# Window attention with a highway layer: fp32 loads by the hardware queue, fp16 conversion and causal masks on GpSimd, VectorE's highway sums kept in PSUM

## The chip, the cores and the metric

The kernel runs on one core of one Trainium2 chip. The metric is the device time of one execution in microseconds (us). A "fast" run is one whose time is within 1.5% of the fastest run of the same kernel; slower runs, which showed a lower granted clock in several cases (the granted clock is the share of TensorE's full clock that the profiler recorded), are called slow and are not compared with fast ones.

## The reference

Attention over a causal window of 128 positions plus 4 "sink" positions at the start of each sequence, and then a highway layer on the 3072 tokens.

```python
# q, k, v: (B=4, H=8, S=768, D=64) fp32; w_h, w_t: (512, 512); b_t: (512)
scores = q @ k.transpose(0, 1, 3, 2) / sqrt(D)
keep   = is_sink | ((rel >= 0) & (rel < 128))
a      = softmax(where(keep, scores, -1e9))
x      = (a @ v).transpose(0, 2, 1, 3).reshape(3072, 512)
Hh     = maximum(x @ w_h, 0)
T      = sigmoid(x @ w_t + b_t)
out    = T * Hh + (1 - T) * x            # (3072, 512) fp32
```

## The kernel before

The work is cut into 24 blocks of 128 rows, six per batch. Per block, `stage_T` transposes q and k, `stage_S` makes the scores and their exponentials `e`, `stage_mask` masks them, `stage_A` multiplies them with V, `stage_X` transposes the result `xh`, and `stage_Mt` and `stage_Mh` are the two matrix products of the highway layer (`tps` for the gate, `hps` for the highway side). Most tiles lie in SBUF; the matrix products are written to tiles in PSUM, where `ps_m` has two buffers for four kinds of tiles. In blocks 2 to 5 of a batch the sinks lie outside the window and are added by `stage_sink`, from two small block-diagonal tiles, `ks_bd` and `vs_bd`. These tiles are filled once per batch by ten small copies within SBUF (`stage_sink_setup`). They are the "sink copies".

```python
    AHEAD = 8
    NV = AHEAD + 3                                   # V ring
    m_ps = tile_pool("ps_m", bufs=2, PSUM)           # shared by tp, tps, hps, sk

    def load(n):                                     # software queue: converts fp32 to fp16
        nc.gpsimd.dma_start(out=qsd, in_=q[b, :, rows, :].transpose([1, 0, 2]))
        nc.gpsimd.dma_start(out=ksd, in_=k[b, :, rows, :].transpose([1, 0, 2]))
    def load_v(n):
        nc.gpsimd.dma_start(out=vt[:, :, 0:D], in_=v[b, :, rows, :].transpose([1, 0, 2]))
    # ... (cut: first loads, weights)
    bt32 = const.tile([1, DM], FP32, tag="bt32")
    nc.sync.dma_start(out=bt32, in_=moe_b_t.unsqueeze(0))          # bias: first DMA of SyncE

    def late_constants():                            # VectorE, in its fixed order
        # ... (cut)
        nc.vector.tensor_scalar_mul(bt16[0:1, :], bt32, 0.5)

    def stage_sink_setup(b):
        for hh in range(2):
            nc.sync.dma_start(out=ks3[rows, :, 4 * hh:4 * hh + NSINK],
                              in_=kT[rows, :, 0:NSINK])
        for h in range(H):
            nc.sync.dma_start(out=vs_bd[b % 2][r:r + NSINK, h // 4, h % 4, :],
                              in_=vt[0:NSINK, 65 * h:65 * h + 65])

    def stage_mask(n):
        for e in es:                                 # two tiles of 128x1024 (128x512 in block 0)
            nc.vector.tensor_tensor(out=ev, in0=ev, in1=m.to_broadcast(...), op=ALU.mult)

    def stage_Mh(n):
        # hps = xT @ wh, four matmuls
        nc.vector.scalar_tensor_tensor(out=dd, in0=hps, scalar=0.0, in1=xh, op0=ALU.max, op1=ALU.subtract)
        nc.vector.scalar_tensor_tensor(out=ee, in0=u, scalar=1.0, in1=dd, op0=ALU.add, op1=ALU.mult)
        nc.vector.scalar_tensor_tensor(out=otok, in0=xh, scalar=2.0, in1=ee, op0=ALU.mult, op1=ALU.add)
        nc.sync.dma_start(out=out[n * P:(n + 1) * P, :], in_=otok)

    with tc.manual_schedule(engines={ENG.PE, ENG.DVE, ENG.Activation}):
        for i in range(-2, NB + 1):
            # stage_sink(i), stage_S(i + 1), stage_A(i), stage_T(i + 2)
            # at each batch's first block: stage_sink_setup; at i == -2: late_constants()
            # loads of block i + 2 + AHEAD
            # stage_mask(i + 1), stage_Mt(i - 1), stage_X(i), stage_Mh(i - 1)
```

The softmax here doesn't subtract the row's maximum and nothing guards it: scores larger than these inputs give would overflow.

## Time and profile before

| | before |
|---|---|
| device time, median of 3 runs (range) | 137.16 us (136.8 to 137.25) |
| span of the profiled execution, granted clock | 134.9 us, 0.979 |
| first matmul of the highway product `hps` of block 0 / block 1 | 23.3 / 28.4 us |
| attention x V of block 2 | 25.3 us |
| `hps` of block 21 / last block | 121.7 / 128.1 us |

These are lines of the page of the kernel before: the busy shares of its engines, and, in 40 equal slices of the span (3.4 us each), tenths of busy time and the bytes moved; then the DMA queues with packets, megabytes and the time their packets took.

```profile
span 134.9 us, 3378 instructions
PE 117.1 (87%) x1312; PEld 73.6 (55%) x1312; DVE 108.5 (80%) x230; ACT 90.4 (67%) x129; POOL 65.7 (49%) x81
...
POOL 6999747889897789979489370000000000000000
...
GB/s 4 111 123 127 160 188 160 155 181 171 154 198 191 196 151 148 152 195 240 192 194 179 193 194 176 38 80 80 6 78 78 63 19 78 78 5 78 78 78 78
...
q0 software_dynamic: 75936, 10.49, 116.0%
q1 hardware_dynamic: 5890, 6.33, 14.6%
```

GpSimd (POOL) does little but issue loads, 0.9 us each, and is finished at 80 us.

The time from one block's `hps` to the next is called the pitch below, and an unusually long one a jump.

### The profile page before, as it was taken

Reading aid. Unit: us, or ns where it says so; the run is one execution under the profiler, and the core shown is the slowest. Engines: PE = TensorE matmul, PEld = TensorE weight load, DVE = VectorE, ACT = ScalarE, POOL = GpSimd, SP = SyncE. Lnnn points to the kernel's source line nnn. Section 1 sums busy time; section 2 is a strip of 40 time slices with the busy share of each in tenths; the row PEclk is TensorE's granted clock in tenths of the full one; section 3 lists DMA queues with packets and bytes.
Section 4 is the critical chain, followed back from the end, with each engine's and each line's share of the span. In section 5 each row is a group of like instructions: output and inputs, shape, how many; then the busy total and the mean of one; then the engine's idle time right before and its main releaser. Section 6 shows DMA issues by size and latency. Waiting matters only on the chain.

```text
span 134.9 us, 3378 instructions
## 1 busy us (share of the span) xinstructions
PE 117.1 (87%) x1312; PEld 73.6 (55%) x1312; DVE 108.5 (80%) x230; ACT 90.4 (67%) x129; POOL 65.7 (49%) x81
## 2 busy tenths in 40 slices
PE   6657939999999899999999899999998999999720
PEld 2225625856864466567565557656653685665300
DVE  6153724789988999899898998998989998999590
ACT  3054843779775977977777788779767977973310
POOL 6999747889897789979489370000000000000000
PEclk9999995999999999999999999999999999999996
DMA  0999999999999999999999999122011101101111
GB/s 4 111 123 127 160 188 160 155 181 171 154 198 191 196 151 148 152 195 240 192 194 179 193 194 176 38 80 80 6 78 78 63 19 78 78 5 78 78 78 78
DMA packets 81841, 17.02 MB, mean 126 GB/s; under 512 B 77729, under 2 KB 78753, under 8 KB 81826
## 3 DMA queue, kind: packets, MB, share of 16 engines
q0 software_dynamic: 75936, 10.49, 116.0%
q1 hardware_dynamic: 5890, 6.33, 14.6%
q8 instruction: 10, 0.16, 0.5%
q14 instruction: 5, 0.04, 0.1%
HBM read 20.97 MB, written 6.29 MB: 202 GB/s over the span
## 4 chain that ended last, share of the span: by engine, by line
DVE 33%; PE 32%; ACT 11%; issue 8%; POOL 7%; DMA 6%; DVEq 0%; POOLq 0%
PE hps L310 12%; ACT e L234 7%; DMA ksd<-in_k_dram 6%; DVE ee L316 6%; DVE otok L319 6%; DVE dd L313 6%; DVE e L247 5%; DVE xh L277 5%; PE tps L298 4%; PE xtp L286 4%; PE av L262 3%; DVE kT L186 3%; PE sk L211 3%; ACT qT L185 3%; POOL qsd L83 2%
## 5 line engine op out<-in xcount | busy, mean ns | idle before, releaser
L234 ACT ACTIVATE e<-sps,ebias 128x1024 f16<-128x1024 f32 (+1 forms) x48 | 47.4, 1039 | 11.2 <-PE sps L231 6.0
L298 PE MATMUL tps<-wt_sb,xT 128*128 128x512 f16 x96 | 25.5, 390 | 0.0
L310 PE MATMUL hps<-wh_sb,xT 128*128 128x512 f16 x96 | 24.7, 379 | 0.7
L83 POOL DMA_DIRECT2D qsd<-in_q_dram x24 | 21.6, 900 | 4.7 <-DMA wh_sb<-in_moe_w_h_dram 1.0
L84 POOL DMA_DIRECT2D ksd<-in_k_dram x24 | 21.4, 893 | 3.1 <-PE tp L182 1.3
L262 PEld LDWEIGHTS <-e 128*128 128x128 f16 x352 | 19.8, 98 | 3.2 <-issue 0.4
L301 ACT ACTIVATE u<-tps 128x512 f16<-128x512 f32 x24 | 14.4, 600 | 9.5 <-PE tps L298 9.5
L247 DVE TENSOR_TENSOR e<-e,mask 128x1024 f16<-128x1024 f16 x32 | 20.5, 682 | 0.0
L185 ACT COPY qT<-tp 128x512 f16<-128x512 f16 x24 | 14.0, 585 | 9.6 <-PE tp L182 9.6
L313 DVE SCALAR_TENSOR_TENSOR dd<-hps,xh 128x512 f16<-128x512 f32 x24 | 16.5, 688 | 4.1 <-PE hps L310 4.1
L186 DVE COPY kT<-tp 128x512 f16<-128x512 f16 x24 | 10.1, 423 | 11.7 <-ACT qT L185 11.7
L316 DVE SCALAR_TENSOR_TENSOR ee<-u,dd 128x512 f16<-128x512 f16 x24 | 16.6, 692 | 2.5
L319 DVE SCALAR_TENSOR_TENSOR otok<-xh,ee 128x512 f32<-128x512 f16 x24 | 16.6, 692 | 0.8
L277 DVE TENSOR_TENSOR xh<-av,rec 128x512 f16<-128x512 f32 x24 | 16.6, 691 | 0.8
L231 PE MATMUL sps<-qT,kT 64*128 64x128 f16 x352 | 15.4, 227 | 2.1 <-DVE kT L186 1.1
L231 PEld LDWEIGHTS <-kT 64*128 64x128 f16 x352 | 10.7, 98 | 9.5 <-issue 6.6
L288 ACT COPY xT<-xtp 128x512 f16<-128x512 f16 x24 | 14.0, 583 | 1.1 <-PE xtp L286 0.9
L298 PEld LDWEIGHTS <-xT 128*128 128x128 f16 x96 | 9.6, 100 | 9.1 <-issue 0.8
L310 PEld LDWEIGHTS <-xT 128*128 128x128 f16 x96 | 9.3, 98 | 8.6 <-issue 1.5
L286 PEld LDWEIGHTS <-xh 128*128 128x128 f16 x96 | 6.4, 101 | 13.4 <-DVE xh L277 11.2
L286 PE MATMUL xtp<-ident,xh 128*128 128x128 f16 x96 | 9.9, 228 | 3.8 <-DVE xh L277 3.8
L180 PE MATMUL tp<-ident,qsd 128*128 128x128 f16 x96 | 10.0, 231 | 2.4 <-DMA qsd<-in_q_dram 2.3
(88 smaller groups left out, 152.9 us busy)
## 6 DMA issues: line engine op xcount, KB each, us to landing
out_dram<-otok SPq DMA_DIRECT2D x24, 256.0 KB
qsd<-in_q_dram POOLq DMA_DIRECT2D x24, 128.0 KB, 7.3
ksd<-in_k_dram POOLq DMA_DIRECT2D x24, 128.0 KB, 7.4
wt_sb<-in_moe_w_t_dram POOLq DMA_DIRECT2D x1, 512.0 KB, 8.4
wh_sb<-in_moe_w_h_dram POOLq DMA_DIRECT2D x1, 512.0 KB, 10.1
v_91<-in_v_dram POOLq DMA_DIRECT2D x3, 128.0 KB, 8.0
v_92<-in_v_dram POOLq DMA_DIRECT2D x3, 128.0 KB, 6.1
v_93<-in_v_dram POOLq DMA_DIRECT2D x2, 128.0 KB, 8.0
```

Source lines behind the costliest of these rows:

```text
L83: nc.gpsimd.dma_start(out=qsd, in_=q[b, :, rows, :].transpose([1, 0, 2]))
L231: nc.tensor.matmul(sps[:, hh, o:o + P], lhsT=kk[rows, hp, :], rhs=qT[rows, hp, :], start=True, stop=True)
L234: nc.scalar.activation(out=e.rearrange("p a b c d -> p a (b c d)"), in_=sps[:, :, 0:2 * np_ * P], func=AF.Exp, bias=ebias, scale=SCALE)
L247: nc.vector.tensor_tensor(out=ev, in0=ev, in1=m.unsqueeze(1).to_broadcast([P, 4, np_ * P]), op=ALU.mult)
L262: nc.tensor.matmul(av[:, g, 2 * hl + hh, 0:_AVN], lhsT=es[g][:, hh, hl, pc, :], rhs=vt[:, 65 * h:65 * h + _AVN], start=first, stop=False, ...
L277: nc.vector.tensor_tensor(out=xh, in0=avh[:, :, 0:D], in1=rec.unsqueeze(2).to_broadcast([P, H, D]), op=ALU.mult)
L286: nc.tensor.transpose(xtp[:, j, :], xh[:, 2 * j:2 * j + 2, :], ident)
L298: nc.tensor.matmul(tps, lhsT=xT[:, kc, :], rhs=wt_sb[:, kc, :], start=False, stop=(kc == NOC - 1))
L310: nc.tensor.matmul(hps, lhsT=xT[:, kc, :], rhs=wh_sb[:, kc, :], start=(kc == 0), stop=(kc == NOC - 1))
L313: nc.vector.scalar_tensor_tensor(out=dd, in0=hps, scalar=0.0, in1=xh, op0=ALU.max, op1=ALU.subtract)
L316: nc.vector.scalar_tensor_tensor(out=ee, in0=u, scalar=1.0, in1=dd, op0=ALU.add, op1=ALU.mult)
L319: nc.vector.scalar_tensor_tensor(out=otok, in0=xh, scalar=2.0, in1=ee, op0=ALU.mult, op1=ALU.add)
```

## The change

The intent is to relieve VectorE. The masks become selects on GpSimd, which frees VectorE of 1.36 us per full block. To make room on GpSimd, the loads go to the hardware queue on SyncE. There the loads fill fp32 staging tiles, and GpSimd casts them to fp16. VectorE's two intermediate sums `dd` and `ee` stay in the PSUM tile `hps`, so that VectorE reads fewer SBUF operands beside GpSimd. The ring of V buffers shrinks from 11 to 6. The core of the diff (constants and the mask tile's shape are cut):

```diff
-    AHEAD = 8
+    AHEAD = 6
+    stage_pool = ctx.enter_context(tc.tile_pool(name="p_stage", bufs=AHEAD))
-    NV = AHEAD + 3
+    NV = 6
     def load(n):
+        for name, src in (("q", q), ("k", k), ("v", v)):
+            t = stage_pool.tile([P, H, D], FP32, tag=name + "32", name=name + "32")
+            nc.sync.dma_start(out=t, in_=src[b, :, rows, :].transpose([1, 0, 2]))
+            stage[name, n] = t
+    def cast(n):
-        nc.gpsimd.dma_start(out=qsd, in_=q[b, :, rows, :].transpose([1, 0, 2]))
-        nc.gpsimd.dma_start(out=ksd, in_=k[b, :, rows, :].transpose([1, 0, 2]))
+        nc.gpsimd.tensor_copy(out=qsd, in_=stage.pop(("q", n)))
+        nc.gpsimd.tensor_copy(out=ksd, in_=stage.pop(("k", n)))      # ScalarE for block 0
+        nc.gpsimd.tensor_copy(out=vt[:, :, 0:D], in_=stage.pop(("v", n)))
...
+    for n in range(AHEAD):
+        load(n)                                # 18 loads on SyncE, ahead of the bias
     bt32 = const.tile([1, DM], FP32, tag="bt32")
     nc.sync.dma_start(out=bt32, in_=moe_b_t.unsqueeze(0))
...
     def stage_mask(n):
-            nc.vector.tensor_tensor(out=ev, in0=ev, in1=m..., op=ALU.mult)
+            # c == 0: VectorE; c == 1: VectorE for the first half; else GpSimd for both halves
+            nc.gpsimd.affine_select(out=ev[:, :, 0, :], in_=ev[:, :, 0, :], ..., **keep_prev)
+            nc.gpsimd.affine_select(out=ev[:, :, 1, :], in_=ev[:, :, 1, :], ..., **keep_cur)
...
-        nc.vector.scalar_tensor_tensor(out=dd, in0=hps, scalar=0.0, in1=xh,
+        nc.vector.scalar_tensor_tensor(out=hps, in0=hps, scalar=0.0, in1=xh,
-        nc.vector.scalar_tensor_tensor(out=ee, in0=u, scalar=1.0, in1=dd,
+        nc.vector.scalar_tensor_tensor(out=hps, in0=u, scalar=1.0, in1=hps,
-        nc.vector.scalar_tensor_tensor(out=otok, in0=xh, scalar=2.0, in1=ee,
+        nc.vector.scalar_tensor_tensor(out=otok, in0=xh, scalar=2.0, in1=hps,
...
+            if i == -2:
+                cast(0); cast(1); load_weights(wt_sb, moe_w_t); cast(2); load_weights(wh_sb, moe_w_h)
+            elif i + 4 < NB:
+                cast(i + 4)                    # ahead of the masks of block i + 1
+            if i + 4 + AHEAD < NB and i > -2:
+                load(i + 4 + AHEAD)
+            elif i == -2:
+                for n in range(AHEAD, AHEAD + 3):
+                    load(n)                    # 9 more loads, ahead of the first sink copies
```

## The prediction

> **What bounds it now.** VectorE. The timeline shows attention x V of block 2 starting at 25.3 us and of block 23 at 122.7: 97.4/21 = 4.64 us per block. VectorE's own work per block, by the groups of instructions: kT 0.42, masks 2x0.68, dd, ee, otok 3x0.69, rec 0.20, xh 0.69 = 4.75 (4.2 for the first block of each six, whose masks are half size). It runs back to back there (18.8 of 20 us busy in the window 100 to 120; PE is as "busy", but its instructions overlap: its starts add up to about 4.2 us per block, estimated from the timeline: scores 0.55, AV 1.02, transposes 0.44+0.23, gate matmuls 1.07, highway matmuls 0.86, sinks 0.46 in a third of the blocks). ScalarE needs 3.8. GpSimd does only DMA issue (0.9 us each) and is done at 80 us. The first 24 us are load and start-up, the last 12 us a tail.
>
> **What changes.**
> 1. Masks leave VectorE for GpSimd: -1.36 us of 4.75 in four blocks of six. VectorE falls to about 3.4 us and stops being the bound by its own work.
> 2. GpSimd gets, per block, four selects of 128x512 and three casts of 128x512. The page shows only 128x128 selects, 0.33 us, starting 0.24 us before the next instruction. Estimate: with 0.05 to 0.1 us fixed, a 128x512 select takes 0.65 to 0.82 us. Casts: the Trainium skill, GPSIMD Engine Reference, "Elementwise - side-by-side cycle accounting", gives 1.03 cycles per element for simple bodies, so an estimate of 0.5 to 0.6 us; no cast is in this trace. Sum 4.1 to 5.1 us per full block, 3.9 to 4.2 averaged over six. Just about hidden.
> 3. Keeping dd and ee in hps takes away two-SBUF-input VectorE ops, which by the Trainium skill (SBUF - State Buffer, "Who interferes with whom") would contend with GpSimd reads. But hps, in a pool of two PSUM buffers shared with tp, tps and sk, is now held until otok, 2.2 us instead of 0.7. The changed program has the next tps (or, before a block with a sink pass, the next tp) wait for VectorE. That is a loop: hps done, dd, ee, otok 2.2, wake-ups 0.25, [tp 0.44], tps 1.07, xtp 0.23, hps 0.86: 4.6 us, 5.1 with tp (two blocks of six). Mean 4.77, against 4.64 now. VectorE's relief is spent on a PSUM wait.
> 4. Loads by the hardware queue: same HBM bytes, about 1 MB moved per block with the store, 215 GB/s at this pace; before moved more than that in the load phase (12 MB read plus stores in 47 us), so it fits. Start-up needs the same 6 MB by about 24 us, plus casts: +-2 us.
> 5. Tail: hps of the last block waits for otok of the one before: about +1 us.
>
> **Sum.** 137.2 + 21x0.13 (2.7) + 1 + 0 = 141; weighed with the chance that start-up gains and that PE fills the waits better, 139.5 us. Range 131 to 150. Chances: faster by over 2% 0.25, within 2% 0.30, slower 0.45.
>
> **What would show each step.** VectorE busy about 82 us instead of 108, with idle time before dd. First gate matmul (or first transpose of q) waiting for otok on VectorE, 0.3 to 0.5 us in each block; block pitch 4.6/5.1 alternating. GpSimd busy 90 to 105 us, selects 0.65 to 0.82, casts 0.5 to 0.6. No growth of VectorE durations. First matmul of block 2's AV still near 25 us.
>
> **What would make it wrong.** Selects at 0.9 us or more, or casts at 0.75: GpSimd is the bound, 145 to 155 us, with AV waiting for GpSimd. Faster GpSimd and hidden hps waits, with a start-up several us shorter: 128 to 132. Small hardware-queue descriptors slow to issue on SyncE: loads would starve the casts.

## More of the kernel before

The loads go through the software queue (q0), and the hardware queue (q1) carries only the stores, the bias and the sink copies.

The columns are start, length, what was issued:

```profile
0.81 0.34 SPq L136 DMA_DIRECT2D bt_145<-in_moe_b_t_dram  x1
7.69 1.99 SPq L200 DMA_DIRECT2D vs_156<-v_91  x3
9.72 1.38 SPq L195 DMA_DIRECT2D ks_154<-kT  x2
11.14 4.32 SPq L200 DMA_DIRECT2D vs_156<-v_91  x5
```

In the first 20 us SyncE issues nothing but the bias, at once, and the ten sink copies of the first batch, as soon as their sources exist. The copies keep SyncE for 7.7 us in this kernel too, but nothing stands behind them.

One period of six blocks is 28.1 us long (`hps` of block 1 at 28.4 us, of block 19 at 112.7 us, divided by 3). A window of 28 us late in the kernel therefore holds one of everything. The columns are the window, its length, then busy time and number of instructions of TensorE, its weight loads, VectorE, ScalarE and GpSimd, then granted clock, DMA share, GB/s:

```profile
90.00:118.00 28.00, 26.91 (x327) 17.36 (x326) 25.73 (x49) 22.10 (x32) 0.00 (x0) 1.00 0.16 58
```

TensorE is busy for 26.9 of 28 us and VectorE for 25.7.

## The result, and the profile after

| | before | after |
|---|---|---|
| device time, median (range) | 137.16 us (136.8 to 137.25) | 160.55 us (160.2 to 162.55) |
| span of the profiled execution, clock | 134.9 us, 0.979 | 158.8 us, 0.88 |
| `hps` of block 0 / block 1 | 23.3 / 28.4 us | 37.0 / 49.0 us |
| attention x V of block 2 | 25.3 us | 41.9 us |
| `hps` of block 21 / last block | 121.7 / 128.1 us | 145.2 / 152.4 us |

The ratio is 1.1753, with a 95% interval of 1.1601 to 1.1905. A ratio here is the mean time of one kernel's fast runs over the mean time of the other's fast runs of the same rounds, so it is not quite the ratio of the medians quoted. The kernel became 17% slower.

The lines of the page after the change that answer to those of before, with the chain of waits added:

```profile
span 158.8 us, 3554 instructions
PE 116.7 (73%) x1312; PEld 75.5 (48%) x1312; DVE 90.7 (57%) x188; ACT 91.0 (57%) x130; POOL 87.9 (55%) x152
...
PE   6430000695669998789999889889998789999740
...
GB/s 121 222 218 212 236 237 217 220 217 151 2 131 220 209 261 257 253 75 61 221 245 265 239 256 267 46 114 266 229 281 113 129 51 26 66 70 66 68 66 66
...
q1 hardware_dynamic: 80770, 25.21, 75.8%
q0 software_dynamic: 1056, 1.05, 4.0%
...
PE 31%; DVE 27%; SPq 20%; ACT 7%; issue 7%; DMA 6%; DVEq 0%
```

VectorE did lose its work (108.5 to 90.7 us busy), and TensorE did the same work in a longer span. A slice is now 4.0 us, and TensorE stands still in slices 4 to 7, about 12 to 28 us. A fifth of the chain is now "SPq", that is, SyncE issuing DMAs. The timeline of SyncE's queue after the change:

```profile
0.81 0.44 SPq L87 DMA_DIRECT2D q_125<-in_q_dram  x1
...
7.31 1.14 SPq L87 DMA_DIRECT2D k_139<-in_k_dram  x1
...
25.01 0.48 SPq L136 DMA_DIRECT2D bt_161<-in_moe_b_t_dram  x1
...
34.68 1.10 SPq L87 DMA_DIRECT2D v_213<-in_v_dram  x1
35.87 3.30 SPq L195 DMA_DIRECT2D ks_170<-kT  x2
39.22 5.10 SPq L200 DMA_DIRECT2D vs_172<-v_94  x8
```

The first issue takes 0.44 us. Once several loads are under way, one takes about 1.14 us and the next starts 1.18 us later. 256 KB per 1.18 us is 222 GB/s, which is what the page's slices show as moved in these microseconds. (Two later loads held SyncE for about 3.6 us each, while the two weight loads of the software queue moved. The first eight loads wait for no earlier transfer in the trace.) So the issue no longer runs ahead: the instruction waits until the queue takes it, and everything behind it in SyncE's order waits too. The bias, formerly issued at 0.81 us, stands behind 18 loads. The first sink copies, formerly issued at 7.69 us, stand behind 27. VectorE works in a fixed order and has the bias' conversion ahead of `kT` of block 1:

```profile
7.87 0.17 DVE L166 MEMSET mask_169<- 4x128 f16 x1
28.14 0.41 DVE L167 TENSOR_SCALAR bt_163<-bt_161 1x512 f16<-1x512 f32 x1 [20.10 <-DMA bt_161<-in_moe_b_t_dram]
28.48 0.41 DVE L186 COPY kT<-tp 128x512 f16<-128x512 f16 x1
```

A 2 KB vector holds up VectorE for 20.1 us, and TensorE with it. Later the late sink copies hold TensorE: the sink matmuls of block 2 wait 2.8 us for `ks`, and attention x V of block 2 starts at 41.9 us instead of 25.3:

```profile
41.92 0.22 PE L272 MATMUL av<-v_95,e 128*128 128x112 f16 x1
```

The other waits of interest, from the view of waits (total, times, longest):

```profile
POOL v_94 L100 <- DMA vs_172<-v_94: 10.4, 2, 7.7
PE tps L306 <- DVE otok L327: 5.9, 13, 0.8
```

The first is a cast of V into a buffer whose old contents the sink copies have yet to read: with the ring cut to 6 buffers, late sink copies hold up GpSimd too. (From e6 on, the runs built on the changed kernel have 9 buffers, e12 excepted.) The second is the PSUM wait that the prediction expected: the gate product `tps` waits for the buffer of `hps` until `otok` is done.

The same 28 us window as before shows how much VectorE was relieved in the steady part (third pair of numbers):

```profile
90.00:118.00 28.00, 25.09 (x300) 16.23 (x297) 20.30 (x39) 21.02 (x31) 19.62 (x34) 1.00 0.95 201
```

VectorE is down from 25.73 to 20.30 us, but TensorE does less in the window, 300 matmul records instead of 327 (a jump of 0.9 us at 101.5 us included): the pitch did not improve.

The difference of the two traces splits into three stretches: `hps` of block 1 comes 20.7 us later; from there to block 21 another 2.8 us are lost (96.1 instead of 93.3 us); from block 21 to the last `hps` 0.9 us more (7.21 instead of 6.35). The sum, 24.3 us, is nearly the difference of the spans, 23.9 us.

The instructions on GpSimd and the sums have nearly the sizes that I had estimated. The groups of instructions (columns after the count: busy us, mean ns of one, idle time before them):

```profile
L258 POOL TENSOR_SCALAR_AFFINE_SELECT e<-e 128x512 f16<-128x512 f16 x40 | 25.4, 634 | 16.6 <-ACT e L234 16.6
...
L327 DVE SCALAR_TENSOR_TENSOR otok<-xh,hps 128x512 f32<-128x512 f16 x24 | 16.5, 686 | 0.8
```

A select takes 0.63 us, and a cast, most often, 0.62 us (0.81 us at most), starting 0.56 us before its successor. This is close to the estimate that I took from the Trainium skill, GPSIMD Engine Reference, section "3.1 Elementwise — side-by-side cycle accounting" (1.03 cycles per element for simple bodies; estimate 0.5 to 0.6 us).

### The profile page after: what moved, and what is told of

Read it like the earlier page. It is cut to its first block, busy times and chain, and to the rows that moved or that the text cites. A ratio compares the mean times of both kernels' runs of the same rounds, so it can differ in the third digit from the quotient of the medians.

```text
span 158.8 us, 3554 instructions
## 1 busy us (share of the span) xinstructions
PE 116.7 (73%) x1312; PEld 75.5 (48%) x1312; DVE 90.7 (57%) x188; ACT 91.0 (57%) x130; POOL 87.9 (55%) x152
## 4 chain that ended last, share of the span: by engine, by line
PE 31%; DVE 27%; SPq 20%; ACT 7%; issue 7%; DMA 6%; DVEq 0%
SPq L87 15%; PE hps L320 11%; PE tps L308 8%; DVE otok L327 7%; DVE hps L324 7%; DVE hps L322 7%; ACT e L234 4%; SPq L200 3%; PE tps L306 3%; DVE kT L186 3%; DMA out_dram<-otok 2%; PE xtp L296 2%; ACT qT L185 2%; DMA vs_172<-v_94 2%; DMA bt_161<-in_moe_b_t_dram 2%
## 5 line engine op out<-in xcount | busy, mean ns | idle before, releaser
L258 POOL TENSOR_SCALAR_AFFINE_SELECT e<-e 128x512 f16<-128x512 f16 x40 | 25.4, 634 | 16.6 <-ACT e L234 16.6
L322 DVE SCALAR_TENSOR_TENSOR hps<-hps,xh 128x512 f32<-128x512 f32 x24 | 16.7, 698 | 23.8 <-PE hps L320 23.8
L256 POOL TENSOR_SCALAR_AFFINE_SELECT e<-e 128x512 f16<-128x512 f16 x32 | 20.3, 634 | 15.5 <-ACT e L234 15.4
L308 PE MATMUL tps<-wt_sb,xT 128*128 128x512 f16 x96 | 25.5, 389 | 0.0
L272 PEld LDWEIGHTS <-e 128*128 128x128 f16 x352 | 20.7, 102 | 3.2 <-issue 0.4
L324 DVE SCALAR_TENSOR_TENSOR hps<-u,hps 128x512 f32<-128x512 f16 x24 | 16.7, 696 | 2.4
L308 PEld LDWEIGHTS <-xT 128*128 128x128 f16 x96 | 9.5, 99 | 16.6 <-issue 8.3
L287 DVE TENSOR_TENSOR xh<-av,rec 128x512 f16<-128x512 f32 x24 | 16.6, 691 | 0.8
L327 DVE SCALAR_TENSOR_TENSOR otok<-xh,hps 128x512 f32<-128x512 f16 x24 | 16.5, 686 | 0.8
L306 PE MATMUL tps<-bt_163,ones_row 128*128 128x512 f16 x24 | 9.3, 388 | 5.9 <-DVE otok L327 5.9
L320 PEld LDWEIGHTS <-xT 128*128 128x128 f16 x96 | 8.6, 98 | 7.7 <-issue 1.9
L167 DVE TENSOR_SCALAR bt_163<-bt_161 1x512 f16<-1x512 f32 x1 | 0.4, 414 | 20.1 <-DMA bt_161<-in_moe_b_t_dram 20.1
L296 PEld LDWEIGHTS <-xh 128*128 128x128 f16 x96 | 7.5, 101 | 7.6 <-DVE xh L287 2.3
L182 PE MATMUL tp<-ident,ksd 128*128 128x128 f16 x96 | 10.0, 231 | 1.4 <-ACT ksd L96 0.8
```

The costliest lines, as they stand in the source:

```text
L256: nc.gpsimd.affine_select(out=ev[:, :, 0, :], in_=ev[:, :, 0, :], pattern=[[0, 4], [-1, P]], **keep_prev)
L258: nc.gpsimd.affine_select(out=ev[:, :, 1, :], in_=ev[:, :, 1, :], pattern=[[0, 4], [1, P]], **keep_cur)
L272: nc.tensor.matmul(av[:, g, 2 * hl + hh, 0:_AVN], lhsT=es[g][:, hh, hl, pc, :], rhs=vt[:, 65 * h:65 * h + _AVN], start=first, stop=False, ...
L308: nc.tensor.matmul(tps, lhsT=xT[:, kc, :], rhs=wt_sb[:, kc, :], start=False, stop=(kc == NOC - 1))
L320: nc.tensor.matmul(hps, lhsT=xT[:, kc, :], rhs=wh_sb[:, kc, :], start=(kc == 0), stop=(kc == NOC - 1))
L322: nc.vector.scalar_tensor_tensor(out=hps, in0=hps, scalar=0.0, in1=xh, op0=ALU.max, op1=ALU.subtract)
```

## The experiments

**Theories at the start.** Theory A: the loss is the bias, a single late DMA that holds VectorE for 20.1 us; put it first and the time comes back. Theory B: the loss is the order of the full queue as a whole, that is, loads ahead of everything else that SyncE issues, so that the next late item holds the kernel as soon as one is mended. Theory C: the loss is bandwidth or GpSimd's own pace: the loads or casts cannot keep up, whatever the order. Theory D: the sums kept in PSUM cost more than the few us of step 3.

Every time is the median of all the run's executions, slow ones included; "ratio" is against the kernel before. 18 kernels ran. The table at the end of this section has them side by side.

### First round: the bias, the sink copies

**e1_bias_first.** The bias' DMA is issued ahead of the loads.

```diff
+    bt32 = const.tile([1, DM], FP32, tag="bt32")
+    nc.sync.dma_start(out=bt32, in_=moe_b_t.unsqueeze(0))
     for n in range(AHEAD):
         load(n)
-    bt32 = const.tile([1, DM], FP32, tag="bt32")
-    nc.sync.dma_start(out=bt32, in_=moe_b_t.unsqueeze(0))
```

> The changed kernel with one line moved: the gate bias load is issued before the block loads instead of after 18 of them. Theory A (the bias behind the loads is the whole start-up loss): VectorE no longer sits idle for 20 us, the first highway matmul starts near 23 us instead of 37, block 2's attention x V near 25 instead of 42, time about 140 us. Theory B (everything small on the SyncE queue is late, the next in line being the ten sink copies behind 27 loads of about 1.18 us each): first highway matmul near 20 to 24 us, but block 2's sink pass still waits for its copies until about 38 to 41 us, time about 155 us. Rival C (start-up is bounded by load bandwidth whatever the order): no gain, 158 to 161.

Measured: 160.23 us, ratio 1.1693 (1.1617 to 1.1769). The 20 us wait for the bias is gone and nothing is gained. (The profiled execution, 162.4 us, was a slow one, so I read only what waits for what from it.) The view of TensorE's timeline shows attention x V of block 1 stopping inside the block, and the sink matmuls of block 2 waiting again:

```profile
16.34 0.28 PE L272 MATMUL av<-v,e 128*128 128x112 f16 x1
26.91 1.58 PE L272 MATMUL av<-v,e 128*128 128x112 f16 x15 [10.29 <-POOL e L258]
...
40.67 1.01 PE L211 MATMUL sk<-qT,ks 128*128 128x128 f16 x8 [8.33 <-DMA ks<-kT]
```

GpSimd's timeline says why the selects of block 1 come at 26 us: they stand behind the casts of block 4, whose loads had not landed.

```profile
23.34 0.62 POOL L94 CAST qsd<-q 128x512 f16<-128x512 f32 x1 [2.95 <-DMA q<-in_q_dram]
24.54 0.62 POOL L98 CAST ksd<-k 128x512 f16<-128x512 f32 x1 [0.58 <-DMA k<-in_k_dram]
25.65 0.62 POOL L100 CAST v<-v 128x512 f16<-128x512 f32 x1 [0.49 <-DMA v<-in_v_dram]
26.22 1.22 POOL L258 TENSOR_SCALAR_AFFINE_SELECT e<-e 128x512 f16<-128x512 f16 x2
```

Theory A falls. The wait moved from the bias to the masks and then to the sink copies.

**e2_sinks_before_loads.** The sink copies are issued before the loads of blocks 6 to 8; the bias stays late.

```diff
-            elif i == -2:
-                for n in range(AHEAD, AHEAD + 3):
-                    load(n)
...
                     stage_sink_setup((i + 2) // NSC)
+                if i == -2:
+                    for n in range(AHEAD, AHEAD + 3):
+                        load(n)
```

> The changed kernel with only the loads of blocks 6 to 8 moved behind the first batch's ten sink copies; the bias stays behind 18 loads. Theory A: nothing that matters, 158 to 161 us. Theory B: VectorE still idles 20 us for the bias, first highway matmul still near 37, but the sink copies land near 32 instead of 44, so block 2's attention x V starts near 36 to 37 instead of 42 and its second half does not wait; about 153 us. Rival C: no gain.

Measured: 158.76 us, ratio 1.1597 (1.1537 to 1.1657). `hps` of block 1 comes 7.2 us earlier than in the changed kernel (41.8 us), and attention x V of block 2 at 38.8 us, but a jump of 9.8 us between two later blocks (65.5 to 75.3 us, twice the usual pitch) takes 5 us of it back.

**e3_both.** Both edits. 

> Both moves: bias first, and the ten sink copies before the loads of blocks 6 to 8 but still behind 18 loads. Theory A: same as bias first, 140. Theory B: sink copies issued from about 25 us and landed near 31, block 2's attention x V near 32, time about 147 to 150 us, and less than either move alone. Rival C: 158 to 161.

Measured: 158.62 us, ratio 1.1589 (1.1516 to 1.1662). Again the start-up improves (`hps` of block 0 at 31.5 us, of block 1 at 36.5), but `hps` of block 2 comes 8.6 us after that, and a later jump grows, to 12.3 us (64.2 to 76.5 us).

**e5_early.** The bias first, then the loads of blocks 0 to 2 only, then the sink copies, then the other loads.

```diff
-    for n in range(AHEAD):
+    for n in range(3):
         load(n)
...
-                    for n in range(AHEAD, AHEAD + 3):
+                    for n in range(3, AHEAD + 3):
                         load(n)
```

> Bias first, then the loads of blocks 0 to 2, then the ten sink copies, then the loads of blocks 3 to 8. Theory A: 140 or worse, as the loads come later. Theory B: sink copies landed by about 17 us; block 2's attention x V at 22 to 26 us, then the pitch of the changed kernel (mean 4.78 us per block, from the PSUM wait), so 139 to 142 us, 1 to 4 per cent slower than the kernel before. Rival C: 150 or more, because the loads of block 3 come 6 us later.

Measured: 155.96 us, ratio 1.1383 (1.1314 to 1.1452). Attention x V of blocks 0 and 1 is as early as in the kernel before (12.6 and 16.0 us), that of block 2 comes at 34.8 us, behind casts of blocks 3 and 4. There are jumps of about 10 us (61.6 to 71.6 us) and 6.6 us (95.3 to 101.9 us) later.

Theory A falls with these runs: the loss is no single wait, and what is delayed is whatever stands behind loads or casts, as B has it. By their times, however, they do not decide between B and C. B's forecasts (155, 153, 147 to 150 and 139 to 142 us) were all missed, by 5 to 14 us, while later jumps remained or grew; C's forecasts (158 to 161 us or no gain, and 150 or more for e5) were met or nearly. Against C spoke only the traces: in e3 `hps` of block 1 comes 12.5 us earlier than in the changed kernel, with the same loads. The same holds of e6, e7, e13 and e16 below: each missed the time that the queue's order had promised and fell where the rival (load bandwidth or GpSimd) had put it. Only e17 decides.

### Second round: the orders on SyncE and GpSimd, and the sums

**e6_boundary.** e5 with each iteration's loads issued after its sink copies, and 9 V buffers instead of 6.

```diff
-    NV = 6
+    NV = 9
...
-            if i + 4 + AHEAD < NB and i > -2:
-                load(i + 4 + AHEAD)
...
                     stage_sink_setup((i + 2) // NSC)
+            if i + 4 + AHEAD < NB and i > -2:
+                load(i + 4 + AHEAD)
```

> The early-sinks kernel, and in every iteration the loads are issued after the sink copies, with nine v buffers instead of six. If the jumps of 10.1 and 6.6 us in the highway pitch at the batch boundaries (61.6 to 71.6, and 95.3 to 101.9 in the early-sinks run; 4.7 elsewhere) come from sink copies queued behind loads that wait for GpSimd, both shrink to about 5 us and the time falls by 6 to 8 us, to 148 to 150. If they come from a burst of loads that merely has to be paid back (bandwidth), they stay or move: 153 to 156. Start-up unchanged: block 2's attention x V still near 35 us.

Measured: 153.43 us, ratio 1.1192 (1.103 to 1.1354). The two later jumps shrink to 7.26 and 7.21 us, not to the 5 us expected.

**e7_pool_order.** e5 with 9 V buffers, as in e6, and GpSimd's order turned round: the masks of block i + 1 first, then the casts, and these one block later (block i + 3); loads after the casts.

```diff
-                cast(2)
-                load_weights(wh_sb, moe_w_h)
-            elif i + 4 < NB:
-                cast(i + 4)
...
                 stage_mask(s)
+            if -2 < i < NB - 3:
+                cast(i + 3)
+                if i == -1:
+                    load_weights(wh_sb, moe_w_h)
+                if i + 3 + AHEAD < NB:
+                    load(i + 3 + AHEAD)
```

> As before, and on GpSimd the masks of block i+1 now come before a cast, and the cast is of block i+3 instead of i+4. If GpSimd's queue order is the rest of the start-up loss (masks of block 1 waiting behind casts of blocks 3 and 4, whose data land at 22 to 28 us), block 1's attention x V starts near 17 us and block 2's near 25 to 28 instead of 35; time 139 to 142 us, i.e. within 1 to 4 per cent over the kernel before, the rest being the PSUM wait (pitch still 4.63 and 5.03 to 5.09). If start-up is bounded by load bandwidth, block 2 stays at 33 us or later and the time at 147 or more.

Measured: 152.71 us, ratio 1.1185 (1.1025 to 1.1344). Attention x V of block 2 comes at 29.7 us. Now the stores stand behind loads: the first one is issued at 45.9 us, and `otok` waits for its buffers. Jumps of 7.7, 5.95 and 9.47 us remain, where the sink copies of the next batches are due.

**e8_ee_sbuf.** e7 with `ee` in SBUF again, so that `hps` is released one VectorE instruction earlier.

```diff
-        nc.vector.scalar_tensor_tensor(out=hps, in0=u, scalar=1.0, in1=hps,
+        nc.vector.scalar_tensor_tensor(out=ee, in0=u, scalar=1.0, in1=hps,
...
-        nc.vector.scalar_tensor_tensor(out=otok, in0=xh, scalar=2.0, in1=hps,
+        nc.vector.scalar_tensor_tensor(out=otok, in0=xh, scalar=2.0, in1=ee,
```

> The Pool-order kernel, with ee written to an SBUF tile, so that hps is held for 1.5 us instead of 2.2; only otok then has two SBUF inputs. PSUM-hold theory: the waits of the first gate matmul or first transpose for VectorE vanish, highway pitch falls from 4.63/5.05 to about 4.2 to 4.5, time 4 to 8 us under the Pool-order run. Rival (the pitch is set by TensorE's own work or by GpSimd): no change, within 1 us.

Measured: 151.07 us, ratio 1.1034 (1.0894 to 1.1174). The waits for the PSUM buffer are gone from the trace, but the eight undisturbed pitches at the end (of `hps` from block 14 on) sum to 37.69 us, against 36.95 in the kernel before and 37.5 in the changed kernel. So the small gain against e7, whose interval overlaps, does not come from the pitch. A miss in that sense.

**e9_both_sbuf.** e7 with `dd` and `ee` both in SBUF.

```diff
-        nc.vector.scalar_tensor_tensor(out=hps, in0=hps, scalar=0.0, in1=xh,
+        nc.vector.scalar_tensor_tensor(out=dd, in0=hps, scalar=0.0, in1=xh,
-        nc.vector.scalar_tensor_tensor(out=hps, in0=u, scalar=1.0, in1=hps,
+        nc.vector.scalar_tensor_tensor(out=ee, in0=u, scalar=1.0, in1=dd,
```

> The Pool-order kernel with both sums in SBUF, as before the change. hps held 0.7 us; ee and otok have two SBUF inputs. If VectorE and GpSimd exclude each other in such instructions, ee and otok grow from 0.69 to 0.9 to 1.3 us and selects and casts stretch too; in full blocks GpSimd's 4.0 us plus 1.4 us leaves a pitch of 5 us or more, 3 to 10 us slower than the ee-in-SBUF run. If they don't, pitch and time equal that run within 1 us, or better it.

Measured: 152.02 us, ratio 1.1123 (1.0959 to 1.1288). The two sums whose inputs are both in SBUF became longer, and so did GpSimd's selects:

```profile
L326 DVE SCALAR_TENSOR_TENSOR ee<-u,dd 128x512 f16<-128x512 f16 x24 | 19.9, 829 | 2.5
L329 DVE SCALAR_TENSOR_TENSOR otok<-xh,ee 128x512 f32<-128x512 f16 x24 | 19.7, 819 | 1.2 <-DMA out_dram<-otok 0.5
...
L258 POOL TENSOR_SCALAR_AFFINE_SELECT e<-e 128x512 f16<-128x512 f16 x40 | 29.1, 732 | 8.8 <-ACT e L234 8.7
```

In the kernel before the same two took 692 ns each; single ones here take up to 1.15 us. In the changed kernel, with one input in PSUM, `otok` took 686 or 687 ns every time. That is the conflict which the Trainium skill, SBUF — State Buffer, section "Who interferes with whom", describes: VectorE's second SBUF port pair is GpSimd's, with an exclusive lock. The trace agrees, and keeping the sums in PSUM does avoid it. What it costs here does not show in the time: e9 is 1 us above e8, inside the intervals, where 3 to 10 us were expected.

### Third round: the parts of the change by themselves

**e10_before_psum.** The kernel before, with only the sums in PSUM (the two lines of the diff of e9, the other way). 

> The kernel before, with only the sums kept in PSUM. PSUM-hold theory of the prediction: hps is held 2.2 us, the next tps or tp waits for otok, and the mean pitch rises from 4.6 to 4.75 or more: 2 to 4 us slower, with TensorE waits for otok in the list of waits. Rival (TensorE's own work and the ScalarE chain set the pitch, the hold fits beside them): within 1 us of the kernel before.

Measured: 139.57 us, ratio 1.0195 (1.0119 to 1.027). This part alone costs 1.6 to 3.7 us. The wait view has the predicted wait, which the kernel before lacks:

```profile
PE tps L296 <- DVE otok L317: 5.6, 13, 0.8
```

The pitches are 4.63 and 5.00 us, the loop that the prediction had worked out (4.6 and 5.1). From block 1 to block 21 they cost 1.3 us (94.68 instead of 93.35), and the tail 0.9 us. Theory D falls: the cost is there but is as small as step 3 said.

**e12_loads_alone.** The changed kernel with the masks back on VectorE and both sums back in SBUF. What is left of the change is the load path: fp32 loads on SyncE, casts on GpSimd. (The diff is that of the change, undone in `stage_mask` and `stage_Mh`.) 

> The changed kernel with the masks back on VectorE and the sums back in SBUF: the load path (hardware queue, GpSimd casts, their orders and buffer counts) alone. If the load path is the cause, nearly the whole loss is here: 155 to 161 us, VectorE idle 20 us for the bias. If the masks on GpSimd are needed for it, it falls to 145 or less.

Measured: 161.36 us, the median of all four; the fast ones took 160.27, 160.91 and 161.81 us, ratio 1.1781 (1.1686 to 1.1876). The whole loss is there without masks or sums. Its profiled execution was a slow one, so I read no times from its trace.

So the load path is enough for the loss. (That the masks cost nothing of their own is not shown by this; see e18.) What remained open was whether it is the order (B) or the pace (C).

### Fourth round: fewer loads ahead

**e13_paced.** e7 with 3 blocks of loads ahead instead of 6, and 6 output buffers instead of 4.

```diff
-    AHEAD = 6
+    AHEAD = 3
-    o_pool = ctx.enter_context(tc.tile_pool(name="p_o", bufs=4))
+    o_pool = ctx.enter_context(tc.tile_pool(name="p_o", bufs=6))
...
                 load_weights(wt_sb, moe_w_t)
+                load(AHEAD)
...
-                    for n in range(3, AHEAD + 2):
-                        load(n)
+                    load(AHEAD + 1)
```

> The Pool-order kernel with the prefetch limited to three blocks ahead of the casts, the sink copies behind four blocks of loads, and six output buffers. If what is left of the loss (12 per cent) is bulk loads in front of stores and sink copies on one queue, the waits of otok for stores (5.4 and 4.3 us in the chain of the Pool-order run) and the late sink copies go, block 2's attention x V comes near 25 to 27 us, and the time is 138 to 142 us. If load bandwidth is the limit, it stays above 147.

Measured: 150.96 us, ratio 1.1043 (1.0975 to 1.1112). The start-up is nearly back: attention x V of blocks 0, 1, 2 at 12.6, 16.4 and 25.5 us, as in the kernel before, though `hps` of block 1 is still 2.6 us late (31.0 us). The rest of the loss lies in jumps of `hps` of 6 to 10 us, where the pitch should be 4.6 or 5. SyncE's timeline at the first sink copies after the start-up:

```profile
44.08 1.61 SPq L87 DMA_DIRECT2D v<-in_v_dram  x1
45.79 0.96 SPq L329 DMA_DIRECT2D out_dram<-otok  x1
46.84 1.67 SPq L195 DMA_DIRECT2D ks<-kT  x2
48.56 5.62 SPq L200 DMA_DIRECT2D vs<-v  x8
54.29 0.38 SPq L87 DMA_DIRECT2D q<-in_q_dram  x1
```

Ten copies of 0.5 to 2 KB keep SyncE for 7.4 us, and no load is issued meanwhile. In the kernel before the first ten copies had taken SyncE as long (7.7 us), so it is not loads on the same queue that make them slow. GpSimd then waits for q, k and v (35.8 us in 31 waits over the kernel, by the view of waits).

**e14_paced_qT.** e13 with `ee` in SBUF and the copy of qT moved from ScalarE to VectorE.

```diff
-        nc.scalar.copy(out=qT, in_=tp[:, 0:NHP, :])
+        nc.vector.tensor_copy(out=qT, in_=tp[:, 0:NHP, :])
```

> The paced kernel, and VectorE's freed time put to use: the qT copy moves from ScalarE to VectorE, and ee goes to SBUF. If the pitch of 4.6 and 5.0 us comes from the chain sink exponential, two exponentials, qT, kT, highway matmul in blocks with a sink pass, and from TensorE in the others, the 5.0 us fall to about 4.7 and the mean to 4.4: 4 to 6 us less than the paced run. If VectorE and GpSimd in each other's way eat it, less than 2 us.

Measured: 151.7 us, ratio 1.1011 (1.0891 to 1.1131); two of the four executions were slow, the fast ones took 149.56 and 151.39 us. No gain that shows; a miss.

**e15_spread.** e13 with 4 blocks ahead, and the ten sink copies of the later batches spread over four blocks (3, 3, 2, 2), still on SyncE.

```diff
+            lo = (0, 3, 6, 8, 10) if b else (0, 10)
+            for o, s in sink_copies(b)[lo[part]:lo[part + 1]]:
+                nc.sync.dma_start(out=o, in_=s)
```

> The paced kernel with four blocks of prefetch, and from the second batch on the ten sink copies spread over four blocks (3, 3, 2, 2) on the same SyncE queue. If the stalls left (highway pitch of 6.4, 5.9, 6.4 and 10.1 us at the batch boundaries of the paced run) come from ten copies of 0.6 us in a row, during which no load is issued, they shrink to 5.0 to 5.5 us each and the time falls by 6 to 9 us, to 142 to 145 us. If the queue is simply full (sum of its issues too long for the pitch), the stalls spread as well and the time falls by less than 3 us.

Measured: 158.05 us, ratio 1.1506 (1.14 to 1.1612). Worse; a miss. The holes in SyncE's loads became small, but the last copies of the second batch are now issued at 67.6 us, behind three more blocks of loads, and one jump of `hps` is 16.6 us (57.4 to 74.1). By the view of waits TensorE now waits 11.2 us for the sink copies `vs`, and the casts on GpSimd 14.6 us for loads; in e13 it was 0.3 and 35.8 us. The copies delay the loads, or the loads delay the copies.

**e16_spread_act.** As e15, but the sink copies are issued by ScalarE, and the copy of qT moves to VectorE.

```diff
+            for o, s in sink_copies(b)[lo[part]:lo[part + 1]]:
+                nc.scalar.dma_start(out=o, in_=s)
```

> The paced kernel with the sink copies of all batches spread over four blocks and issued by ScalarE, and the qT copy moved from ScalarE to VectorE to make room; sums still kept in PSUM. The SyncE queue then holds loads and stores only. If that queue is the cause, loads run on without the 6 us holes, block 2's attention x V comes near 24 to 27 us, no pitch exceeds 5.3 us, and the time is 137 to 142 us, level with the kernel before or up to 4 per cent behind, as the PSUM hold predicts. If load bandwidth or GpSimd is the cause, it stays above 145.

Measured: 147.28 us, the median of all four (fast ones 146.94 to 147.31), ratio 1.0735 (1.066 to 1.081). Of the 14 us that e13 loses against before, this gains back 4. Its trace (from a slow execution, 151.1 us) still has holes of about 6 us in SyncE's loads. In this program each DMA of the hardware queue waits for the landing of an earlier one, eight before it, ScalarE's included. I had only argued that this makes the holes, but the trace names it, in the view of SyncE's own waits (total, times, longest):

```profile
SPq L87 <- DMA vs<-v: 24.1, 9, 5.9
```

The loads wait for the copies that ScalarE, busy with its own work, issues late. No run tested what the time would be without these waits.

### Fifth round: no sink copies on the queue, and the masks alone

**e17_no_sinks.** e13 without any sink copies. The result is wrong (relative error 0.11): the sink tiles stay zero. All compute instructions stay.

```diff
     def stage_sink_setup(b):
-        # two ks copies, eight vs copies
+        return
```

> The paced version (e13_paced, 150.96 us) with the ten sink copies of each batch left out altogether; the result is wrong on purpose (the sinks are zero where they should be copied), all compute instructions stay. If what is left of the loss is the sink copies standing between the loads on SyncE and its queue: the four jumps of 6 to 10 us go, pitch 4.63/5.05 throughout, 139 to 142 us. If it is the load bandwidth or GpSimd (casts waiting for loads whatever else is on the queue): over 146 us, with casts on GpSimd still waiting for DMA of q, k or v.

Measured: 139.0 us in the fast runs (138.7 to 139.03), ratio 1.0174 (1.008 to 1.0268). Forty small copies were worth 12 us. (The profiled execution was slow, 156 us, but its pitches are regular, without a jump.) With casts of all loads, masks and sums all as in the change, the kernel is as fast as e10, the kernel before with its sums in PSUM (ratios 1.0174 and 1.0195). Theory C falls: neither the bandwidth of the hardware queue nor GpSimd's pace is what was lost.

**e18_masks_swq.** The kernel before with the masks alone on GpSimd; loads by the software queue, sums in SBUF.

```diff
     def stage_mask(n):
-            nc.vector.tensor_tensor(out=ev, in0=ev, in1=m..., op=ALU.mult)
+            nc.gpsimd.affine_select(...)          # as in the change
...
-    with tc.manual_schedule(engines={ENG.PE, ENG.DVE, ENG.Activation}):
+    with tc.manual_schedule(engines={ENG.PE, ENG.DVE, ENG.Activation, ENG.Pool}):
...
+            if 0 <= s < NB:
+                stage_mask(s)                     # ahead of the loads of the iteration
```

> The kernel before with one part of the change only: the causal masks as selects on GpSimd, loads still by the software queue from GpSimd, sums in SBUF as before. VectorE loses 1.36 us per full block. If VectorE was the bound: 133 us or less. If three chains were balanced (my reading now): TensorE back to back in the odd blocks still gives 4.55, so 134 to 138. If GpSimd's DMA issue (0.9 us each, three loads a block, 2.7 us) before or between the selects (2.5 us) delays the masks: attention x V waits for GpSimd in the first half and the time is 138 to 143.

Measured: 153.11 us, ratio 1.1252 (1.1101 to 1.1404). I had expected 143 at most. TensorE's timeline shows one wait, in block 1, and GpSimd's shows what its selects stood behind:

```profile
34.43 1.58 PE L274 MATMUL av<-v,e 128*128 128x112 f16 x15 [17.81 <-POOL e L260]
```

```profile
31.92 0.93 POOL L84 DMA_DIRECT2D ksd<-in_k_dram  x1
32.78 0.94 POOL L91 DMA_DIRECT2D v<-in_v_dram  x1
33.66 1.30 POOL L260 TENSOR_SCALAR_AFFINE_SELECT e<-e 128x512 f16<-128x512 f16 x2
```

In program order the first selects come after the issue of 30 loads (blocks 0 to 9, 0.9 us each). It is the same fault as in the change, on another engine: work that is needed at once, behind loads that are needed much later. After that wait the pitches from block 1 to block 20 are those of the kernel before to within 0.1 us, but for one that is 0.6 us longer, so removing the masks from VectorE bought nothing there.

**e19_sinks_once.** e13 with a correct result and no sink copies on SyncE. The sink rows of V of all batches are loaded once by eight software-queue loads, the constant column is set by eight copies from ScalarE, and the sink columns of K are copied by VectorE.

```diff
+    def load_sinks():
+        for h in range(H):
+            nc.gpsimd.dma_start(out=vs_all[r:r + NSINK, :, h // 4, h % 4, 0:D],
+                                in_=v[:, h, 0:NSINK, :].transpose([1, 0, 2]))
+            nc.scalar.dma_start(out=vs_all[r:r + NSINK, :, h // 4, h % 4, D:D + 1],
+                                in_=twos.unsqueeze(2))
...
-            nc.sync.dma_start(out=ks3[rows, :, 4 * hh:4 * hh + NSINK],
-                              in_=kT[rows, :, 0:NSINK])
+            nc.vector.tensor_copy(out=ks3[rows, :, 4 * hh:4 * hh + NSINK],
+                                  in_=kT[rows, :, 0:NSINK])
```

> The paced version (150.96 us; 139.0 without sink copies, wrong result) with a correct result but no sink copies on SyncE: the sink rows of V of all four batches are loaded once at the start by eight software-queue loads from GpSimd (0.9 us of issue each, 7 us on GpSimd behind the weights), the constant column by eight small copies from ScalarE, and the sink columns of K by two small VectorE copies per batch. If the sink copies on SyncE were the rest of the loss: 139 to 143 us, pitch 4.63/5.05 without jumps. If the gain of the wrong version came from something else that the missing copies did (timing of masks, zeros): over 146. The 7 us on GpSimd at the start may delay the masks of block 1 or the casts of block 3 by some us.

Measured: 142.69 us, correct, ratio 1.038 (1.0305 to 1.0454). The steady part has no jump left: the pitches are 4.63 to 5.03 us, and 95.1 us pass from block 1 to block 21, 1.8 us more than before. `hps` of block 1 comes 3.6 us late, and that is my own doing. ScalarE's timeline:

```profile
11.20 6.87 ACTq L162 DMA_DIRECT2D vs<-twos  x8
18.11 2.12 ACT L239 ACTIVATE e<-sps,ebias 128x1024 f16<-128x1024 f32 x2 [6.39 <-DMA vs<-twos]
```

Eight tiny copies, issued while the loads fill the queue, took ScalarE 6.87 us, and the exponentials of block 1 waited behind them.

**e20_masks_swq_paced.** e18 with 3 blocks of loads ahead instead of 8. (The text below says "7 fewer" loads; by the program it is 15 fewer, and the "22" is 30.)

```diff
-    AHEAD = 8
+    AHEAD = 3
-    sd_pool = ctx.enter_context(tc.tile_pool(name="p_sd", bufs=AHEAD))
+    sd_pool = ctx.enter_context(tc.tile_pool(name="p_sd", bufs=AHEAD + 3))
-    NV = AHEAD + 3
+    NV = AHEAD + 6
```

> The masks alone on GpSimd with software loads (153.1 us: the first selects stand behind 22 loads of 0.9 us, attention x V of block 2 at 40.8 us instead of 25.3, every later pitch as before) with 3 blocks of loads ahead instead of 8, so that the selects of block 1 stand behind 7 fewer loads. If the loss of that run was this order: about 137 to 141 us, attention x V of block 2 at 26 to 30 us, pitch 4.55/5.0. If VectorE was the bound all along and the masks' removal pays once the order is mended: under 134. If GpSimd has too much per block (5.2 us against 4.7): over 143 with pitch above 5.

Measured: 137.19 us, ratio 1.0051 (0.999 to 1.0113): the same as before. Attention x V of block 2 comes at 26.9 us. The 28 us window, to be held against those of before and after:

```profile
90.00:118.00 28.00, 26.84 (x327) 17.28 (x325) 20.82 (x40) 21.95 (x33) 22.84 (x31) 1.00 1.23 125
```

VectorE has 4.9 us less to do in 28 us, and TensorE does exactly as much as before, 327 matmul records in 26.84 us. That is the answer on the masks: VectorE's relief is real and worth nothing. Why is read from the traces, not shown by a run. TensorE is as full as it was, as far as its modelled busy time tells. And what idle time it shows in the steady part is a wait for VectorE's `xh`, the same in the kernel before (first line) and in e20 (second):

```profile
PE xtp L286 <- DVE xh L277: 3.8, 11, 0.9
PE xtp L298 <- DVE xh L289: 3.8, 11, 0.9
```

In e20's chain of waits (from 96 to 110 us) that wait closes a loop of `hps`, `dd`, `ee`, `otok`, `rec`, `xh`, `xtp` and the next `hps`, 4.5 to 4.6 us a block, in which VectorE and TensorE take turns. The masks are not in it, so taking them away does not shorten it. (In the kernel before, the chain runs partly through this loop and partly through the masks, at the same pitch.) No version beat the kernel before.

| run | what it is | median us | ratio |
|---|---|---|---|
| after | the change | 160.55 | 1.175 |
| e1, e2, e3 | bias first; sink copies earlier; both | 160.23, 158.76, 158.62 | 1.169, 1.160, 1.159 |
| e5, e6, e7 | orders on SyncE and GpSimd | 155.96, 153.43, 152.71 | 1.138, 1.119, 1.119 |
| e8, e9 | e7, one or both sums in SBUF | 151.07, 152.02 | 1.103, 1.112 |
| e12 | load path alone | 161.36 | 1.178 |
| e13, e14 | 3 blocks ahead; and qT on VectorE | 150.96, 151.7 | 1.104, 1.101 |
| e15, e16 | sink copies spread: SyncE; ScalarE | 158.05, 147.28 | 1.151, 1.074 |
| e17 | e13 without sink copies (wrong result) | 139.0 | 1.017 |
| e19 | e13, sinks once and off SyncE | 142.69 | 1.038 |
| e18, e20 | masks alone; with fewer loads ahead | 153.11, 137.19 | 1.125, 1.005 |
| e10 | sums in PSUM alone | 139.57 | 1.020 |

## Why the prediction was right or wrong

The prediction was wrong: 139.5 us with a range of 131 to 150, and measured 160.55. The direction had the largest single chance (slower, 0.45), but the size was outside the range. That the direction came out is no merit of the reasoning: it was forecast for a PSUM wait, which alone costs 2.6 us (e10), and came from the load path.

**The step that failed is step 4**, "Loads by the hardware queue: same HBM bytes [...] so it fits. Start-up needs the same 6 MB by about 24 us, plus casts: +-2 us." The start-up measured +20.7 us at `hps` of block 1, and the test that the prediction itself had named, "First matmul of block 2's AV still near 25 us", gave 41.9 us. I had checked that the bytes fit, and they do: e17 carries them all in 139.0 us. I had not checked the order in which the queue takes them. By moving the loads to SyncE, the change put 18 loads ahead of the bias, 27 ahead of the sink copies and, on GpSimd, casts of later blocks ahead of the masks of earlier ones. In the kernel before, SyncE's queue was nearly empty and every small transfer went as soon as its source was there. e1 shows that this is no matter of a single item (the bias moved, 160.23 us), e12 that the load path by itself is enough for it (161.36 us), e5, e7 and e13 together that other orders and fewer loads ahead bring most of the start-up back (attention x V of block 2 at 34.8, 29.7 and 25.5 us), and e17 and e19 that the rest of the loss was the sink copies on the same queue (139.0 us, wrong result; 142.69 us, correct).

**Step 1, VectorE is the bound**: its arithmetic was right (-1.36 us per full block) but the reading behind it was not. e20 relieves VectorE of the masks and is no faster (ratio 1.0051). By the traces TensorE's instructions fill the block as well (26.9 of 28 us busy before, 26.84 in e20), and the loop through `hps` and `xh` does not hold the masks; which of the two limits was not tested. I had estimated TensorE at about 4.2 us per block from starts in the timeline and so thought that it had slack. It has little: the pitch of e20, 4.5 to 5.03 us, is that of the kernel before (4.5 to 5.0 us), longer where a sink pass falls. VectorE was busy 90.7 us in the changed kernel, where about 82 was predicted.

**Step 2, GpSimd's costs**, was near, each figure just outside its range: selects 0.63 us and casts 0.62 us (predicted 0.65 to 0.82 and 0.5 to 0.6 us), busy 87.9 us (predicted 90 to 105).

**Step 3, the PSUM wait**, was right as a mechanism, and in one trace half the size: the wait of `tps` for `otok` is there, 13 times, the pitches are 4.63 and 5.00 us (predicted 4.6 and 5.1), and the sums alone cost 2.6 us by the medians of e10 (137.0 to 139.6 us). The Sum's 2.7 us from block 1 to block 21 measured 1.3 us in e10's trace and 2.8 in the changed kernel, 0.9 of that in one jump.

**Step 5, the tail**, was right: 0.9 us (predicted about 1).

**The list of dangers** named "small hardware-queue descriptors slow to issue on SyncE: loads would starve the casts". At the start that is not what happened: the loads moved 222 GB/s, and it was everything else that starved behind them. At the later batches something like it did: in e13 the ten sink copies keep SyncE for 7.4 us, and the casts wait 35.8 us for loads over the kernel. The danger was named and given no weight in the sum.

**What stays open.** e17 and e19 take the sink copies off SyncE and with them both effects: the issue time in which no load starts, and the late landing of copies behind loads. Which of the two costs how much was not separated by a run. The waits lean one way in e13 (casts wait 35.8 us for loads, TensorE 0.3 us for copies) and show both in e15 (14.6 and 11.2 us). In e16 the holes are named by the trace of a slow execution, and no run removed them. The fast time of e17 has no trace of its own. The difference between before and e20 (medians 136.69 and 137.19 us) is within the interval.

## What to carry to other kernels

When loads move to another queue, write down what that queue carried before and where each item now stands in its order; a total of bytes that fits says nothing about a 2 KB vector behind 18 loads. A queue that is kept full needs its prefetch depth chosen so that small, urgent transfers do not meet it, or needs them elsewhere: the loads that were harmless on a queue of their own cost 17% here, in front of everything else. And before relieving the busiest engine, ask whether the work that goes is part of the loop that sets the pitch, and what the next engine would do with the time: at 26.9 of 28 us busy on TensorE, VectorE's 4.9 us were worth nothing.

## What the Trainium skill lacked or had wrong

- DMA: Bandwidth & Descriptors, section "Issuing engines are not separate DMA queues", calls the issuing time "usually small relative to the DMA itself". Here a 256 KB load held SyncE 0.44 us on an empty queue and about 1.14 us on a full one, as long as its bytes need at 222 GB/s (18 loads from 0.81 to 25.0 us, among them two of about 3.6 us beside the weight loads). Ten sink copies of 0.5 to 2 KB held it 7.4 us (e13), and 7.7 us in the kernel before, where no load was on its queue. The page doesn't say that the issuing engine is held back once the queue is full.
- The same page, section "Issuing engine by pattern", calls the hardware path generally faster and gives it for simple loads and stores. The load path alone, on the hardware queue, cost 17.8% (e12) by the order it imposed, and nothing that shows once the order was mended and the small copies were gone (e17 at 1.017 against e10 at 1.020). Perfetto Trace Analysis, section "DMA Optimizations", advises to give inputs and outputs separate issuing engines, but no page says that small SBUF copies behind loads on one engine's hardware queue wait for them, or what it costs.
- DMA: Bandwidth & Descriptors, section "Queues, rings and completion order", says that descriptors are consumed in ring order on each SDMA engine; the runs do not speak against it (bias issued at 25.01 us behind 18 loads, landed by 28.1 us), but the page gives no figure for the landing time of a small transfer behind loads. Here it was 3.1 us.
- GPSIMD Engine Reference, section "3.1 Elementwise — side-by-side cycle accounting", is near for the cast: 1.03 cycles for each of 512 elements, at the 1.2 GHz of its example, are by estimate 0.44 us, and casts of 128x512 took 0.62 us, 0.56 us from one start to the next. It has no time for a select with a computed pattern (its section 7 has cycles per element for compare-and-select bodies in general): 0.63 us for 128x512, 0.59 us from start to start, and 0.71 to 0.73 us on average where VectorE reads two SBUF operands beside it (e9).
- SBUF — State Buffer, section "Who interferes with whom", is borne out, and the sizes that it gives (6.8 and 1.5 times slower, by issue order) are of instructions that it does not name: VectorE's sum of two SBUF operands took 0.69 us alone, 0.82 to 0.83 us on average and 1.15 us at worst beside GpSimd (e9), and 0.686 us every time with one operand in PSUM (the changed kernel). In e20, with selects but no casts on GpSimd, the same sums of two SBUF operands took 0.69 us every time, and the selects 0.70 us on average and 1.14 at most.
